# A gated attention block on one core: second-pass output weights loaded a quarter per period, VectorE side work spread anew

## The chip, the cores and the metric

The kernel runs on one core of one Trainium2 chip. Times are device microseconds of that core. The time before is the median of three runs. One further execution was profiled; its trace gives the durations used below. In the trace PE is TensorE (matmuls) and PEld its weight loads, DVE is VectorE, ACT is ScalarE, POOL is GpSimd; SPq is the queue of SyncE, which issues most of the transfers.

## The reference

```python
xn = _layernorm(x)                                  # x: [2048, 640]
# A: 32 heads of 192, the last W = 512 of 2048 cached keys and values
q = xn @ wq                                         # [640, 6144]
p = softmax(q_h @ k_h.T * 192 ** -0.5)              # per head h
s = concat_h(p @ v_h) @ wo                          # [6144, 640]
# B: gated linear unit, 1536 wide
g = silu((sigmoid(xn @ w_gate) * (xn @ w_up)) @ w_down)
return x + s * g
```

Inputs and output are bf16.

## The kernel before

Three stages follow each other, and TensorE works through nearly all of the time.

**Stage B** (about the first 196 us) normalises x and computes g, which is stored to DRAM as `gB_d`.

**Attention** runs in 16 passes `r` = 0 to 15 (`last` = 15). Pass `r` takes two pairs of heads (group `g`) and one half `pi` of the rows, two blocks of 512. In each pass 16 steps `k` compute scores (`stage_s`, L649): six matmuls into one of two PSUM bank pairs, `k % 2` choosing the pair, then one exponential on ACT (L661). So step `k + 2` can't start before the exponential of step `k` has read its banks. Between the steps TensorE does the query projections of the next pass (L571, in `query_slots`), which DVE takes out of PSUM (L592, L605). Then eight `stage_pv` calls (L663) multiply by the values; DVE normalises into `o_st` (L677, L678), a DMA turns it and `store_o` (L691) writes it to `oT_d`. The last pass puts a `stage_pv` behind every second score step, on two PSUM bank pairs.

`phase_s` (L791) is the hand-written schedule of side work in the attention stage: what follows step `k` of pass `r`. It holds the scale factors (`set_scale`, a maximum sent through DRAM to all partitions by two GpSimd transfers, and `set_scale2`, L212, five small DVE instructions that read it back), the sums of absolute values (`abs_v`, L716, on ACT, four per group, one per value tile), and the preparation of the first output weights.

**Output projection** (from about 695 us): `s` is the [2048, 6144] attention output times `wo`. The inner dimension is cut into two halves `h`, 24 chunks of 128 each; h = 0 is the first pass, h = 1 the second. Per half, the product is done by a seven-product scheme on 2 x 2 blocks. The weight side needs seven operands `ops[h][0..6]` of 128 x 3840 elements: four quarters loaded from `wo` (n = 0, 4, 5, 3, by `load_ops`, L696, 960 KB each) and scaled by DVE (`scale_op`, L701), and differences of them (`sum_op`, L704). The row side needs per period four "quads" (A11, A12, A21, A22, 384 KB each, `load_quads`, L760), scaled (L772, ACT) and combined (`sum_quad`, L776, four DVE instructions at L782 to L789).

There are 16 periods `m` (loop at L986): 0 to 7 with h = 0, 8 to 15 with h = 1. A period is seven products of 12 matmuls each (L935), in the order S1, S2, A12, S3, A11 of the next period, S4, A22; the A11 of period 0 stands ahead of the loop. They use the operands 1, 2, 3, 4, 0, 5, 6. Three results per period are added by DVE (L953; L961 and on in the second pass), one is copied by ACT (L942). A product that goes on in a PSUM bank must wait for the DVE result that reads it: A22 of a period waits for the result behind S3.

After a row tile has its first-pass sum in `acc`, `prep` (L921) turns it into x + acc * g in two DVE steps: `gated` (L919, with a row of `gB_d`) and an addition (L927, with a row of x). The two rows, 160 KB each, are brought by `pair_load` (L910) into three pairs of buffers; the second step of a `prep` issues the pair three tiles on. `todo` (L969 to L977) says which scalings, differences and preparation steps a period gets; `side(m, count)` takes `count` of them at five fixed places of the period: two behind S1, one behind S2, one ahead of the S4 result, one behind it, up to four at the end.

All engines run their queues in order, SPq included: at L989 to L994 period 0 issues the quads of period 2, then the four quarters for h = 1, then the first three pairs of gate and x rows.

Of the kernel before, what the change touches and what calls it, by code (L numbers as in the profile page):

```python
# [10 lines left out]
BF16 = mybir.dt.bfloat16  # L11
# [6 lines left out]
def kernel(  # L18
# [13 lines left out]
    nc = tc.nc  # L32
# [660 lines left out]
                oT[:].rearrange("p (q j) e -> p q j e", q=TQ),  # L693
            )

    def load_ops(h):  # L696
        c = 2 * KB * h
        for n, k, d in ((0, 0, LEFT), (4, 0, RIGHT), (5, KB, RIGHT), (3, KB, LEFT)):
            nc.sync.dma_start(ops[h][n].bitcast(BF16), wo_r[:, c + k:c + k + KB, d])  # L699

    def scale_op(h, n):  # L701
        nc.vector.tensor_scalar(ops[h][n], ops[h][n].bitcast(BF16), o_up, None, op0=ALU.mult)

    def sum_op(h, n, part_=None):  # L704
        B11, T1, T2, B21, T3, B22, T4 = ops[h]
        cs = slice(0, KB) if part_ is None else slice(part_ * KB // 2, (part_ + 1) * KB // 2)
        a, b, c = (t[:, cs, :] for t in ((T1, T3, B11), (T2, B22, T1), (T3, B22, T3), (T4, B21, T2))[n])
        nc.vector.tensor_tensor(a, b, c, ALU.subtract)
# [7 lines left out]
    def abs_v(g, n):  # L716
        col = g * NV + n
        nc.scalar.activation(
            v_abs[g // (NG - 1)], v_t[g, n // 2][n % 2][:, :, 0:DH], AF.Abs, accum_out=v_sum[:, col:col + 1])
# [17 lines left out]
    def weights(g, c):  # L737
        scale_w(g, c)
        sum_w(g, c, nc.gpsimd.tensor_tensor, nc.gpsimd.tensor_copy)
        n = g * NCD + c + 3  # L740
        if n < NG * NCD:
            load_raw(n // NCD, n % NCD, nc.gpsimd)
# [48 lines left out]
    def phase_s(r, pi, g, k, q_list, pv_list):  # L791
        for j in q_after.get(k, ()) if q_list else ():
            q_list[j]()
        if r == 0 and k in scale_s:
            scale_raw(1, scale_s[k], on_act=False)
            second_w(scale_s[k])
        if pi == 0 and g + 1 < NG:
            if k == 2 and g > 0:
                load_k((g + 1, 0))
            elif k == 12:  # L800
                scale_k((g + 1, 0))
                load_k((g + 1, 1))
        if pi == 1 and g + 1 < NG:
            if k == 7:
                scale_k((g + 1, 1))
            elif k == 13:
                turn_k((g + 1, 0))
        n = 3 * (g - 1) + k // 2
        if pi == 1 and k == 8:
            for n in range(3 * g, min(3 * g + 3, NWO)):  # L810
                load_wo(n)
        elif pi == 0 and g > 0 and k in (1, 3, 5) and n < NWO:
            abs_wo(n)
        if pi == 1 and g < NG - 1 and k in (1, 3, 4, 5):
            abs_v(g, (1, 3, 4, 5).index(k))
        if r == last - 3 and k == 7:
            set_scale(wo_sum[:], mx_rows[0], mx_o, 1)
        if r == last - 2:
            if k == 7:
                set_scale2(mx_rows[0], mx_o, o_up, o_down)  # L820
            elif k in (9, 11, 13):
                scale_op(0, (0, 4, 5)[(k - 9) // 2])
        if r == last - 1:
            if 5 <= k < 9:
                abs_v(g, k - 5)
            elif k == 10:
                set_scale(v_sum[:], mx_rows[1], mx_v, 2)
            if k in (9, 11, 13):
                sum_op(0, (k - 9) // 4, (k - 9) // 2 % 2)
        if r == last:  # L830
            if k == 0:
                sum_op(0, 1, 1)
            elif k == 2:
                sum_op(0, 2)
            elif k == 13:
                scale_op(0, 3)
            elif k == 14:
                sum_op(0, 3)
            elif k == 4:
                set_scale2(mx_rows[1], mx_v, v_up, v_down)  # L840
                nc.vector.tensor_tensor(descale, v_down, o_down, ALU.mult)
            if k % 2:
                q, x = pv_list.pop(0)
                stage_pv(q, *x)
            if 5 <= k < 9:
                scale_quad(0, ("A21", "A22", "A11", "A12")[k - 5], nc.vector)
            elif 9 <= k < 13:
                sum_quad(0, k - 8)
            if k in (5, 9, 11, 13, 15):
                store_o(1)  # L850

    held = []
    for r, (pi, g) in enumerate(runs):
        s_list = [(i, pp, c) for i in range(2) for pp in range(G) for c in range(KC)]
        pv_list = held + [(r, (i, pp, h)) for i in range(2) for pp in range(G) for h in range(2)]
        q_list = query_slots(r + 1, False, (0, 1), (2, 3), (2, 3, 1)) if r < last else []
        ring[:] = [0, 1, 2, 3]
        bank_order[:] = [1, 0] * 5 if r == last else [0, 1, 2, 3, 0, 2, 1, 0]
        if r == last - 1:
            bank_order[4:] = [1, 0]  # L860
        for k, x in enumerate(s_list):
            stage_s(r, *x, k)
            if k == 0:
                store_o(0 if r < last else 1)
            phase_s(r, pi, g, k, q_list, pv_list)
        if pi == 1 and g + 1 < NG:
            turn_k((g + 1, 1))
        if r == last - 1:
            for m in range(2):
                load_quads(m)  # L870
        if r == last - 1:
            held[:] = pv_list[-2:]
            del pv_list[-2:]
        for k, (q, x) in enumerate(pv_list):
            stage_pv(q, *x)
            if k in (5, 7):
                store_o(2)
            if pi == 0 and 1 <= g < NG - 1 and k in (2, 4):
                weights(g + 1, 2 + k // 2)
            if pi == 1 and g + 2 < NG and k in (1, 3, 5):  # L880
                weights(g + 2, k // 2)
        if pi == 1 and g + 1 < NG:
            for pp in range(G):
                load_v(g + 1, pp, nc.sync)
        if r == last - 3:
            load_ops(0)
    store_o(0)

    lctx.close()
# [31 lines left out]
    def prep(n, step):  # L921
        t = order[n]
        gate, x_sb = gx_rows[0, t]
        if step == 0:
            gated(acc[t][:], acc[t][:], gate)
        else:
            nc.vector.tensor_tensor(acc[t][:], acc[t][:], x_sb, ALU.add)  # L927
            if n + 3 < len(order):
                pair_load(0, n + 3, first)
# [36 lines left out]
        elif (i, d) in ((0, RIGHT), (1, LEFT)):  # L966
            nc.gpsimd.dma_start(of[t * P:(t + 1) * P, :], o_sb)  # L967

    todo = {2: [lambda n=n: scale_op(1, n) for n in (0, 4, 5, 3)]}  # L969
    for m in (3, 4):  # L970
        todo[m] = [lambda n=n: sum_op(1, n) for n in (2 * m - 6, 2 * m - 5)]
    preps = [(n, j) for n in range(2 * 8) for j in range(2)]
    for m, count in {1: 4, 5: 6, 6: 6, 7: 6, 8: 2, 9: 2, 10: 2, 11: 2, 12: 2}.items():
        for _ in range(count):
            n, j = preps.pop(0)
            todo.setdefault(m, []).append(lambda n=n, j=j: prep(n, j))
    assert not preps  # L977

    def side(m, count=1):
# [6 lines left out]
    for m in range(NP):  # L986
        X, Y, Z = (4, 5, 6) if m % 2 == 0 else (0, 1, 2)
        more = m + 1 < NP
        if m + 2 < NP:  # L989
            load_quads(m + 2)  # L990
        if m == 0:
            load_ops(1)
            for n in range(3):
                pair_load(0, n, first)  # L994
        if 8 <= m < NP - 1:
            for i in range(2):
                pair_load(1, 2 * (m - 7) + i, more_rows)
        product(m, Y, "S1", 1, True)
        if more:
            scale_quad(m + 1, "A21", nc.scalar)  # L1000
        keep(Y, p5s[:])
        side(m, 2)
        product(m, X, "S2", 2, False)
        if more:
            scale_quad(m + 1, "A11", nc.scalar)
        keep(X, u2s[:])
        side(m)
        product(m, Z, "A12", 3, True)
        result(m, 0, LEFT, Z, p1s)
        if more:  # L1010
            scale_quad(m + 1, "A22", nc.scalar)
            scale_quad(m + 1, "A12", nc.scalar)
        product(m, X, "S3", 4, False)
        result(m, 1, RIGHT, X, p5s)
        if more:
            sum_quad(m + 1, 1)
            sum_quad(m + 1, 2)
            sum_quad(m + 1, 3)
            product(m + 1, 4 - X, "A11", 0, True)
            keep(4 - X, p1s[:])  # L1020
        side(m)
        product(m, Y, "S4", 5, False)
        result(m, 0, RIGHT, Y, u2s)
        side(m)
        product(m, X, "A22", 6, False)
        result(m, 1, LEFT, X, None)
        if more:
            sum_quad(m + 1, 4)
        side(m, 4)
        if m == 7:  # L1030
            for i in range(2):
                pair_load(1, i, more_rows)
# [29 lines left out]
```

## Time and profile before

| | us |
|---|---|
| median of 3 runs | 893.09 (892.0 to 897.35) |
| profiled execution | 893.61 |
| its span in the trace | 891.8 |
| PE busy | 873.5 (98%) |
| DVE busy | 669.8 (75%) |
| ACT busy | 577.6 (65%) |
| POOL busy | 231.2 (26%) |

The profiled execution took 1.8 us more than its span. By stretches of the span (busy us of each engine, granted TensorE clock, bytes moved):

| stretch, us | PE | DVE | ACT | clock | GB/s |
|---|---|---|---|---|---|
| 200 to 600 (attention) | 400.0 | 295.8 | 316.7 | 1.00 | 180 |
| 690 to 700 | 8.55 | 5.66 | 3.95 | 1.00 | 149 |
| 700 to 710 | 10.00 | 5.00 | 5.97 | 1.00 | 309 |
| 710 to 720 | 7.87 | 0.00 | 5.07 | 1.00 | 323 |
| 720 to 730 | 4.04 | 7.37 | 1.08 | 0.66 | 298 |
| 730 to 740 | 10.00 | 8.18 | 6.84 | 1.00 | 253 |
| 740 to 860 | 120.0 | 102.3 | 77.1 | 1.00 | 200 |

A row of a timeline gives start, length, engine, line, operation, tiles and how many instructions it merges; the bracket says how long the engine stood idle before it and what it waited for. The chain of waits is the path followed back from the last instruction; each row is a stretch of it.

### The profile page before, as it was taken

How to read it: one execution, taken by the hardware profiler on the slowest of the kernel's cores; microseconds unless marked ns; L12 is line 12 of the kernel's file. 1: busy time of each engine (PE TensorE's matmuls, PEld its weight loads, DVE VectorE, ACT ScalarE, POOL GpSimd, SP SyncE). 2: the span in 40 equal slices, each digit the busy share in tenths (PEclk: the TensorE clock that was granted, in tenths of full speed). 3: DMA queues.
4: the chain of work that ended last, by engine and by line, in shares of the span. 5: the costliest groups of instructions: out<-in, count | busy, mean ns of one | idle time of the engine just before them, and what ended most of it. 6: DMA issues, size and time to landing. Idle time of an engine off the chain costs nothing.

```text
span 891.8 us, 18752 instructions
## 1 busy us (share of the span) xinstructions
PE 873.5 (98%) x7576; PEld 564.1 (63%) x7593; DVE 669.8 (75%) x1086; ACT 577.6 (65%) x693; POOL 231.2 (26%) x326
## 2 busy tenths in 40 slices
PE   9999999999999999999999999999999969999998
PEld 5545454557756756766766765775766647777775
DVE  4879947777777777677777777778788458789986
ACT  4333346774896896896896887877456536666662
POOL 0050212662424524523623622621000000000000
PEclk9999999999999999999999999999999989999999
DMA  9993485229799889779979879879977894468641
GB/s 276 270 279 91 106 126 119 83 64 190 130 218 177 150 220 209 126 212 205 170 185 228 150 174 189 153 153 294 174 196 185 249 304 141 131 225 301 194 150 38
DMA packets 246791, 161.34 MB, mean 181 GB/s; under 512 B 158576, under 2 KB 231664, under 8 KB 246704
## 3 DMA queue, kind: packets, MB, share of 16 engines
q1 hardware_dynamic: 238160, 132.90, 61.8%
q0 software_dynamic: 8544, 27.24, 13.9%
q8 instruction: 59, 0.97, 0.5%
q14 instruction: 28, 0.23, 0.1%
HBM read 93.65 MB, written 30.41 MB: 139 GB/s over the span
## 4 chain that ended last, share of the span: by engine, by line
PE 93%; DVE 3%; SPq 2%; DMA 1%; ACT 1%; issue 1%; DVEq 0%; ACTq 0%
PE ps_all L571 20%; PE ps_all L671 19%; PE ps_all L935 19%; PE ps_all L657 18%; PE ps_all L469 11%; PE ps_all L517 6%; SPq L699 1%; PE ps_all L382 1%; DMA kraw<-gB_d 1%; DMA x_sb<-in_A_x_dram 0%; SPq L913 0%; DVE o_st L678 0%; DVE arm L919 0%; ACT E L661 0%; DVE qT L605 0%
## 5 line engine op out<-in xcount | busy, mean ns | idle before, releaser
L661 ACT ACTIVATE E<-ps_all 128x1024 bf16<-128x1024 f32 x256 | 251.6, 1021 | 123.0 <-PE ps_all L657 122.4
L657 PE MATMUL ps_all<-qT,kT 64*128 64x512 bf16 x1536 | 197.6, 376 | 0.6 <-ACT E L661 0.5
L671 PEld LDWEIGHTS <-E 128*128 128x128 bf16 x2048 | 169.5, 98 | 11.4 <-issue 11.4
L671 PE MATMUL ps_all<-v_sb,E 128*128 128x193 bf16 x2048 | 174.9, 247 | 1.4 <-DVE o_st L678 1.4
L605 DVE TENSOR_TENSOR qT<-ps_all,qp 128x512 bf16<-128x512 f32 x176 | 116.9, 688 | 48.3 <-PE ps_all L571 40.8
L592 DVE COPY qp<-ps_all 128x512 f32<-128x512 f32 x150 | 100.6, 687 | 49.4 <-PE ps_all L571 49.4
L657 PEld LDWEIGHTS <-kT 64*128 64x128 bf16 x1536 | 83.7, 94 | 80.3 <-issue 6.0
L935 PEld LDWEIGHTS <-mid 128*128 128x128 f16 x996 | 98.1, 99 | 47.2 <-issue 8.3
L678 DVE TENSOR_TENSOR o_st<-ps_all,rden 128x768 bf16<-128x768 f32 x128 | 122.5, 957 | 4.4
L571 PE MATMUL ps_all<-mid,arm 64*128 64x512 f16 (+1 forms) x840 | 105.7, 376 | 0.6 <-DVE qp L592 0.6
L571 PE MATMUL ps_all<-mid 64*128 64x512 f16 (+1 forms) x840 | 104.5, 376 | 0.6 <-ACT qp L590 0.5
L571 PEld LDWEIGHTS <-mid 64*128 64x128 f16 x840 | 47.8, 94 | 45.0 <-issue 2.0
L571 PEld LDWEIGHTS <-arm 64*128 64x128 f16 x840 | 47.8, 94 | 44.8 <-issue 1.3
L772 ACT ACTIVATE mid<-mid,w_sc 128x1536 f16<-128x1536 bf16 x41 | 63.4, 1571 | 0.0
L967 POOL DMA_DIRECT2D out_dram<-arm x14 | 7.6, 540 | 206.7 <-DVE arm L963 206.7
L240 ACT ACTIVATE mid<-mid,w_sc 128x1536 f16<-128x1536 bf16 x37 | 58.2, 1572 | 0.6
L935 PE MATMUL ps_all<-mid 128*128 128x320 f16 x312 | 46.6, 305 | 8.1 <-DVE acc L953 8.1
L226 POOL DMA_DIRECT2D mid<-in_A_wq_dram x80 | 48.1, 606 | 23.9 <-DVE mid L262 22.4
L474 ACT ACTIVATE sig_sb<-ps_all 128x512 bf16<-128x512 f32 x48 | 28.0, 596 | 40.1 <-PE ps_all L469 37.1
L517 PE MATMUL ps_all<-wd_sb,hT_sb 128*128 128x128 bf16 (+1 forms) x377 | 52.4, 298 | 0.4
L935 PE MATMUL ps_all<-arm,mid 128*128 128x320 f16 x348 | 51.4, 300 | 0.0
L475 DVE TENSOR_TENSOR hT_sb<-ps_all,sig_sb 128x512 bf16<-128x512 f32 x48 | 32.5, 683 | 23.0 <-PE ps_all L469 11.7
(160 smaller groups left out, 1047.4 us busy)
## 6 DMA issues: line engine op xcount, KB each, us to landing
oT_d<-oT SPq DMA_DIRECT2D x64, 384.0 KB, 5.2
mid<-oT_d SPq DMA_DIRECT2D x45, 384.0 KB, 4.0
mid<-in_A_wq_dram POOLq DMA_DIRECT2D x80, 192.0 KB, 6.7
arm<-in_A_wo_dram SPq DMA_DIRECT2D x16, 480.0 KB, 5.8
v_sb<-in_A_v_cache_dram SPq DMA_DIRECT2D x28, 192.0 KB, 6.0
kraw<-in_A_k_cache_dram SPq DMA_DIRECT2D x26, 192.0 KB, 4.1
mid<-in_A_wq_dram POOLq DMA_DIRECT2D x9, 480.0 KB, 6.7
kT<-oT_d SPq DMA_DIRECT2D x11, 384.0 KB, 4.5
```

Of the source, the lines that this page charges most:

```text
L240: nc.scalar.activation(raw.bitcast(F16), raw, AF.Copy, scale=w_up)
L469: nc.tensor.matmul(gu[:, i, :], lhsT=w[:, c, f * P:(f + 1) * P], rhs=xnT[s][:, c, :], start=(c == 0), stop=(c == NCD - 1),)
L517: nc.tensor.matmul(oB_ps[:, d0:d0 + dsz], lhsT=hT_sb[:, f, q * P:(q + 1) * P], rhs=wd_sb[:, f, d0:d0 + dsz], start=(f == 0), stop=(f == NF ...
L571: nc.tensor.matmul(ps_all[:, b, :], lhsT=w(r, c), rhs=x[r, c, :], start=(first and k == 0), stop=(k == len(cs) - 1), skip_group_check=True,)
L592: nc.vector.tensor_copy(dst, part(b))
L605: nc.vector.tensor_tensor(q_out(i, u, pp), part(b), t, ALU.add)
L657: nc.tensor.matmul(ps[:, b, :], lhsT=kT[h, c * PC + j, :], rhs=qT_t[r][i, j][h, pp, :], start=(j == 0), stop=(j == PC - 1),)
L661: nc.scalar.activation(E_t[r, i, pp][:, c, :, :], ps, AF.Exp, scale=scale_qk)
L671: nc.tensor.matmul(o_ps[:, q // 2, q % 2, 0:DH + 1], lhsT=E[:, c, h, q * P:(q + 1) * P], rhs=vt[:, c, 0:DH + 1], start=(c == 0), stop=(c = ...
L678: nc.vector.tensor_tensor(o_st[:, :, h * DH:(h + 1) * DH].rearrange("p (b i) d -> p b i d", b=2), o_ps[:, :, :, 0:DH], rden[:].to_broadcas ...
L772: eng.activation(t, t.bitcast(BF16), AF.Copy, scale=v_up)
L935: nc.tensor.matmul(ps_all[:, b, 0:DN], lhsT=a[:, c, :], rhs=w[:, c, :], start=(start and c == 0), stop=(c == KB - 1), skip_group_check=True,)
```

## The change

The four quarters for h = 1 are no longer issued together in period 0: `load_op(h, j)` issues one, and periods 0 to 3 call it once each, behind the quads and, in period 0, behind the first gate and x rows. Their scaling moves from period 2 (all four) to periods 2, 3, 4 and 5, one each; the four differences from periods 3 and 4 (two each) to periods 4, 5, 6 and 7. The 32 preparation steps, before 4, 6, 6, 6, 2, 2, 2, 2, 2 in periods 1, 5, 6, 7, 8, 9, 10, 11, 12, become 4, 4, 4, 2, 2, 4, 4, 1, 1, 2, 2, 1, 1 in periods 1 to 13.

In the attention stage `set_scale2` for the weights moves from step 7 to step 0 of pass 13; the four `abs_v` of pass 14 move from steps 5 to 8 to steps 3 to 6; and the scaling and difference that make `ops[0][3]` and `ops[0][6]` move from steps 13 and 14 of pass 15 to behind that pass's last `stage_pv`. The first pass's weights are loaded as before. No instruction is added or removed.

```diff
-    def load_ops(h):
-        c = 2 * KB * h
-        for n, k, d in ((0, 0, LEFT), (4, 0, RIGHT), (5, KB, RIGHT), (3, KB, LEFT)):
-            nc.sync.dma_start(ops[h][n].bitcast(BF16), wo_r[:, c + k:c + k + KB, d])
+    op_parts = (0, 0, LEFT), (4, 0, RIGHT), (5, KB, RIGHT), (3, KB, LEFT)
+
+    def load_op(h, j):
+        n, k, d = op_parts[j]
+        c = 2 * KB * h + k
+        nc.sync.dma_start(ops[h][n].bitcast(BF16), wo_r[:, c:c + KB, d])
...
         if r == last - 2:
-            if k == 7:
+            if k == 0:
                 set_scale2(mx_rows[0], mx_o, o_up, o_down)
...
         if r == last - 1:
-            if 5 <= k < 9:
-                abs_v(g, k - 5)
+            if 3 <= k < 7:
+                abs_v(g, k - 3)
...
-            elif k == 13:
-                scale_op(0, 3)
-            elif k == 14:
-                sum_op(0, 3)
...
+        if r == last:
+            scale_op(0, 3)
+            sum_op(0, 3)
         if pi == 1 and g + 1 < NG:
             for pp in range(G):
                 load_v(g + 1, pp, nc.sync)
         if r == last - 3:
-            load_ops(0)
+            for j in range(len(op_parts)):
+                load_op(0, j)
...
-    todo = {2: [lambda n=n: scale_op(1, n) for n in (0, 4, 5, 3)]}
-    for m in (3, 4):
-        todo[m] = [lambda n=n: sum_op(1, n) for n in (2 * m - 6, 2 * m - 5)]
+    todo = {2 + j: [lambda n=part_[0]: scale_op(1, n)] for j, part_ in enumerate(op_parts)}
+    for n in range(4):
+        todo.setdefault(4 + n, []).append(lambda n=n: sum_op(1, n))
     preps = [(n, j) for n in range(2 * 8) for j in range(2)]
-    for m, count in {1: 4, 5: 6, 6: 6, 7: 6, 8: 2, 9: 2, 10: 2, 11: 2, 12: 2}.items():
-        for _ in range(count):
-            n, j = preps.pop(0)
+    for m, count in enumerate((0, 4, 4, 4, 2, 2, 4, 4, 1, 1, 2, 2, 1, 1)):
+        for n, j in preps[:count]:
             todo.setdefault(m, []).append(lambda n=n, j=j: prep(n, j))
+        del preps[:count]
...
         if m == 0:
-            load_ops(1)
             for n in range(3):
                 pair_load(0, n, first)
+        if m < len(op_parts):
+            load_op(1, m)
```

## The prediction, made before the changed kernel had run

> **What bounds the kernel now.** The page first: TensorE is busy for 98% of the span and 93% of the chain that ended last is PE, so only a gap of TensorE, or work that makes one, changes the time. The stretches (table above) leave one place, 690 to 730. The chain of waits in order of time, columns start, length, what, shows it:
>
> ```profile
> 688.06 1.21 DVE mid L702
> ...
> 690.35 2.07 DVE mid L708
> ...
> 693.56 1.49 PE ps_all L671 x16
> 695.05 9.79 PE ps_all L935 x72
> 704.87 0.45 ACT p1s L942
> 705.32 1.25 SPq L699
> 706.56 0.05 issue
> 706.61 4.23 SPq L699
> 710.89 3.65 SPq L699
> 714.53 0.04 issue
> 714.58 3.08 SPq L913
> ...
> 719.13 5.06 DMA kraw<-gB_d
> ```
>
> The end hangs on DVE's scaling and difference at 688 to 692, and then on SPq: three of the four quarters (L699) keep it for 10 us, and the gate rows (L913) wait behind them. The timeline has what TensorE lost:
>
> ```profile
> 619.82 1.26 PE L571 MATMUL ps_all<-mid,arm 64*128 64x512 f16 x10 [0.61 <-DVE qp L592]
> ...
> 693.56 1.49 PE L671 MATMUL ps_all<-v_sb,E 128*128 128x193 bf16 x16 [1.45 <-DVE o_st L678]
> ...
> 722.56 0.89 DVE L919 SCALAR_TENSOR_TENSOR acc<-acc,w_sc,v_sb 128x640 f32<-128x640 f32 x1 [14.71 <-DMA v_sb<-gB_d]
> ...
> 725.96 3.36 PE L935 MATMUL ps_all<-mid 128*128 128x320 f16 x12 [8.09 <-DVE acc L953]
> 729.11 3.83 PE L935 MATMUL ps_all<-arm,mid 128*128 128x320 f16 x24
> ```
>
> Three gaps: 0.61, 1.45 and 8.09 us. The third is one in-order queue: DVE stands at L919 (the first `gated`) for 14.71 us, the result that A22 of period 1 needs is queued behind it, and TensorE waits. After it the granted clock is 0.51 in 726 to 730: the next three products take from 725.96 to 732.77, 6.81 us, against 4.89 at the steady 1.63 of one product (starts at 734.40, 736.03, 737.66). That is 1.92 more. From there to 860 TensorE has no gap.
>
> **Gate rows ahead of the quarters.** The last quad of period 0 leaves SPq at 703.04; with 1.45 us won before, 701.6. The first gate row follows at once. Gate rows took 5.1 to 7.9 us to land, so it is there at 706.7 to 709.5. When must it be? A22 of period 1 is due at 716.08 + 1.63 - 1.45 = 716.3, and DVE has two `gated` (0.88), one addition (0.82) and two results (0.49) before it, 3.56: the row may land as late as 712.7. Three microseconds of cover even with the slowest row, so I take the whole gap and its slow clock as gone, 8.09 + 1.92 = 10.0. If the row took the 11.5 us of a quarter, 0.4 would be left.
>
> **Quarters later.** Quarter j is now issued in period j behind that period's quads and scaled two periods on, at its start. A period is 11.41 us (the ACT copies that end it stand at 752.53, 763.95, 775.36), so 22.8 less some 4 for the issue are left; quarters landed after 8.4 to 11.5. Cost nothing, with 7 us to spare. SPq: quads of period 3 move ahead of three quarters, while quads of later periods get a quarter and up to four rows behind or before them. One period then moves four quads of 393 KB, one quarter of 983 KB and four rows of 164 KB, 3.21 MB in 11.41 us, 281 GB/s; period 0 moves 3.54 MB, 310 GB/s. The stretch moved 311 to 338 GB/s at 710 to 722, so period 0 fits barely and the quads of period 3, due at 718, have about two us of slack behind it.
>
> **DVE's periods.** Every first-pass period has four `sum_quad` (0.95) and three results (0.49), 5.3. With a scaling 1.21, a difference 2.15 and a preparation pair 1.70, the new periods hold: 1: 8.7; 2 and 3: 9.9; 4 and 5: 10.3; 6 and 7: 10.8. From 8 on the base is 9.4 (three results of 0.49 + 0.55 + 0.49, one of 0.54 + 0.49, the quads' 3.8); one or two steps make 10.3 to 11.1, and 11.1 is what periods 8 to 12 had without a gap. All stay under 11.41. Periods 6 and 7 have the least cover of the new ones; the longest block ahead of a result is 3.4 (scaling and difference in 4 and 5), and period 3 had 4.3 before without a gap. Cost nothing, up to 1 a period if the cover fails.
>
> **Last `scale_op` and `sum_op` of the first pass.** L702 and L708 leave DVE ahead of the `o_st` that TensorE waited for; without them `o_st` ends at about 691.95 and the next `stage_pv` is due at 692.1. The 1.45 go. They now stand behind the last `o_st`, 694.8 to 698.2. The scaled quarter is wanted by the fourth product, 693.6 + 3 x 1.63 = 698.5 (done 696.0), the difference by the eighth, 705.0, and the first result behind them is due at 700.6. Covered by 2.4 us; without cover it would cost the same 1.5.
>
> **`set_scale2` at step 0 of pass 13.** Five instructions, 0.96 us, leave a DVE that was late at 619. The 0.61 go. In the new place DVE stood idle for 1.33 us (before the L592 at 605.85), and the row it reads was issued by GpSimd at 596.31 and lands 3.7 us later, 600.0, 4.5 us ahead. Cost nothing.
>
> **`abs_v` two steps earlier.** This adds a wait. The value tiles of the last group are loaded only after pass 13:
>
> ```profile
> 641.20 3.41 SPq L177 DMA_DIRECT2D v_sb<-in_A_v_cache_dram  x4
> 641.98 1.02 ACT L661 ACTIVATE E<-ps_all 128x1024 bf16<-128x1024 f32 x1 [0.70 <-PE ps_all L657]
> 643.77 1.02 ACT L661 ACTIVATE E<-ps_all 128x1024 bf16<-128x1024 f32 x1 [0.76 <-PE ps_all L657]
> ...
> 646.35 0.83 ACT L718 ACTIVATE mid<-v_sb 128x768 bf16<-128x768 bf16 x1
> ```
>
> Step 3's exponential ends at 643.0; the first tile took 4.3 us, so it lands at 645.5. ACT stands 2.5 us with the exponential of step 4 queued behind. Followed on (0.85 per `abs_v`, 0.95 per exponential, all in before's times): step 4 ends at 647.4, and step 6's matmuls, 646.29 before, overwrite its banks: 1.1 late. ACT then alternates both, 1.8 each, up to step 7; step 8's exponential ends at 653.7, and step 10's matmuls, 652.78 before, start then: 0.9 late. Beyond it ACT needs 0.95 a step against TensorE's 1.73 and catches up. Ends: 2.5 if TensorE loses all that ACT does; -0.5 if the tiles land in time, since before step 10 had a wait of 0.47 of this sort. I take 0.9, followed through the queue. Here a rule speaks against the edit. The Trainium skill, "DMA: Bandwidth & Descriptors", Rules for kernel authors, says to issue a transfer early and wait for it late; moving the reader forward does the opposite. The same page ("Anatomy of one DMA") gives 2.0 us + bytes / 436e3, fitted to GpSimd's transfers; for 192 KB that is an estimate of 2.5 us, the tile would be there at 643.7 and the loss nearly nothing, 11.9 or so off in all. The trace's 4.3 for this very transfer decides.
>
> **The sum.** 0.61 + 1.45 + 10.0 - 0.9 = 11.2 off 893.61 (span 891.8 and 1.8 around it) is 882.4. The median of before is 0.5 below the profiled execution: 882.0.
>
> **Rivals.** (1) *Gates still late.* Transfers already under way (stores, quads) hold the rows back beyond 712.7, and part of the third gap stays. For it: the transfer engines are at a share of 0.98 to 1.16 in 698 to 722. Against: the rows landed in 5.1 to 7.9 in that very crowd. A row 15 us late leaves 4 us: 886. A page bears on the clock alone: by "TensorE: Matmul & The Clock Gate", Part 1, only idle time above about 3.4 us drops the clock; here 1.45 left it at 1.00 and 8.09 did not, and no row lies between.
>
> (2) *DVE becomes the bound* in periods 4 to 7, where differences and preparations meet. 10.3 to 10.8 of 11.41 are taken; if handovers eat the rest, four periods lose 0.5 to 1: 884 to 886.
>
> (3) *Transfers become the bound: slower.* Place: periods 0 to 3, where quarters now run beside quads and rows instead of in TensorE's gap. If the queue brings less than 281 GB/s, the quads come late, ACT can't scale them, and TensorE waits each period. It decides at 223 GB/s: 14.4 us a period, four times 3.0, eats 12; at 210 GB/s the kernel takes about 897. For it: 740 to 760 moved only 138 GB/s. Against: that was all that was asked; the full stretches moved 311 and more.
>
> That the change doesn't do what it says can be left aside: both instruction lists hold the same instructions per engine, and the gates stand ahead of the first quarter.
>
> **Numbers.** About 1% (9 us; 884.2) is what a measurement here tells from no change. Forecast, 881 to 884: 0.80. Rival 1: 0.10. Rival 2: 0.06. Rival 3: 0.04. Low end 880.0: no cost for `abs_v` and before's best run, 892.0. High end 886.0: rivals 1 and 2. Faster: 0.80 + 0.06 from rivals that cost little = 0.86; slower 0.03 of rival 3; the rest within 1%.
>
> **What would show it.** No PE gap at L671 near 692 and none beside L953 in period 1; clock 1.00 in 690 to 740; L919's first wait under 3 us; SPq with L913 before the first quarter; ACT waiting 2 to 2.5 us for `v_sb` in pass 14, and about 1 us of PE gaps at L657 behind it. Wrong: a wait of DVE for `arm` or `op` at a scaling, of ACT at L772 for quads, or PE gaps of A22 in periods 4 to 7.

## The result and the profile after

The changed kernel takes 881.46 us (median of 4 runs, 881.04 to 882.14) against 893.68 for the kernel before (4 runs, 892.0 to 897.35): a ratio of 0.9858, 95% interval 0.9827 to 0.989. Its profiled execution took 881.57 with a span of 879.8, 12.0 shorter than the span before.

The list of TensorE's waits from pass 13 to the end (who waited for whom, us in total, times, longest) had four lines before, 8.1, 1.4, 0.6 and 0.5 us. After the change one is left:

```profile
PE ps_all L657 <- ACT E L661: 1.2, 1, 1.2
```

The stretches (columns: from and to, length, busy us and count of PE, PEld, DVE, ACT, POOL, then the granted clock, the share of the transfer engines, GB/s) show 690 to 730 filled and the clock full:

```profile
690.00:700.00 10.00, 10.00 (x90) 7.98 (x88) 6.70 (x8) 5.47 (x7) 0.00 (x0) 1.00 0.78 186
700.00:710.00 10.00, 10.00 (x75) 7.20 (x74) 7.49 (x10) 5.97 (x8) 0.00 (x0) 1.00 1.04 337
710.00:720.00 10.00, 10.00 (x76) 7.22 (x74) 7.62 (x11) 5.97 (x8) 0.00 (x0) 1.00 1.09 367
720.00:730.00 10.00, 10.00 (x76) 7.19 (x75) 7.01 (x11) 5.97 (x7) 0.00 (x0) 1.00 0.92 303
```

The timeline of SPq and DVE at the start of the projection answers to the rows of L699, L913 and L919 before. Lines have moved by two: L915 is the gate row, L917 the x row, L701 a quarter, L768 a quad, L921 `gated`:

```profile
701.26 0.50 SPq L915 DMA_DIRECT2D v_sb<-gB_d  x1
...
704.97 0.33 SPq L917 DMA_DIRECT2D kraw<-in_A_x_dram  x1
706.06 0.38 SPq L701 DMA_DIRECT2D arm<-in_A_wo_dram  x1
706.99 3.39 SPq L768 DMA_DIRECT2D mid<-oT_d  x4
707.48 0.88 DVE L921 SCALAR_TENSOR_TENSOR acc<-acc,w_sc,v_sb 128x640 f32<-128x640 f32 x1 [1.49 <-DMA v_sb<-gB_d]
```

The six rows leave within some 4 us, one quarter follows, then the quads of period 3. DVE's wait for the first gate row fell from 14.71 to 1.49 us, and no PE gap follows it. In the chain of waits (start, length, what) one row stands where the kernel before left TensorE at 704.84 and came back to it at 725.96:

```profile
693.19 177.68 PE ps_all L937 x1308
```

From the first product to 870.87 the chain is TensorE alone. The last 8.9 us of the span are the second pass's last results on DVE, as long as before.

What is new stands in pass 14, in the timeline of ACT and PE:

```profile
644.69 0.84 ACT L720 ACTIVATE mid<-v_sb 128x768 bf16<-128x768 bf16 x1 [2.76 <-DMA v_sb<-in_A_v_cache_dram]
...
645.53 1.00 ACT L661 ACTIVATE E<-ps_all 128x1024 bf16<-128x1024 f32 x1
...
646.59 0.82 PE L657 MATMUL ps_all<-qT,kT 64*128 64x512 bf16 x6 [1.18 <-ACT E L661]
```

The first `abs_v` waits 2.76 us for its value tile, the exponential of step 4 comes behind it, and step 6's matmuls wait 1.18 for that.

### The profile page after: what moved, and what is told of

It reads as the page before. It is cut to its first block, busy times and chain, and to the rows that moved or that the text cites. A ratio compares the mean times of both kernels' runs of the same rounds, so it can differ in the third digit from the quotient of the medians.

```text
span 879.8 us, 18750 instructions
## 1 busy us (share of the span) xinstructions
PE 870.9 (99%) x7576; PEld 563.3 (64%) x7593; DVE 669.7 (76%) x1086; ACT 577.2 (66%) x693; POOL 231.1 (26%) x326
## 4 chain that ended last, share of the span: by engine, by line
PE 97%; ACT 1%; DVE 1%; DMA 0%; issue 0%; SPq 0%; DVEq 0%
PE ps_all L571 20%; PE ps_all L937 20%; PE ps_all L671 20%; PE ps_all L657 19%; PE ps_all L469 11%; PE ps_all L517 6%; PE ps_all L382 1%; ACT E L661 0%; DMA x_sb<-in_A_x_dram 0%; ACT mid L720 0%; DVE arm L921 0%; DVE arm L965 0%; ACT qp L590 0%; DVE arm L963 0%; DVE qT L605 0%
## 5 line engine op out<-in xcount | busy, mean ns | idle before, releaser
L671 PEld LDWEIGHTS <-E 128*128 128x128 bf16 x2048 | 169.5, 98 | 9.9 <-issue 9.8
L671 PE MATMUL ps_all<-v_sb,E 128*128 128x193 bf16 x2048 | 174.9, 247 | 0.0
L937 PE MATMUL ps_all<-op,mid 128*128 128x320 f16 x336 | 48.2, 299 | 0.0
```

The costliest lines, as they stand in the source:

```text
L671: nc.tensor.matmul(o_ps[:, q // 2, q % 2, 0:DH + 1], lhsT=E[:, c, h, q * P:(q + 1) * P], rhs=vt[:, c, 0:DH + 1], start=(c == 0), stop=(c = ...
L937: nc.tensor.matmul(ps_all[:, b, 0:DN], lhsT=a[:, c, :], rhs=w[:, c, :], start=(start and c == 0), stop=(c == KB - 1), skip_group_check=True,)
```

## The experiments

Up to pass 13 all kernels here are the same program, yet pass 13 starts anywhere from 602.8 to 604.0 us in their traces. So a difference of a microsecond between two medians can lie ahead of the change. Each trace was therefore cut at the same four instructions: the first score matmul of passes 13, 14 and 15, and the first product; the last stretch ends with the span. All in us, from the start columns of the PE timelines:

| kernel | pass 13 | pass 14 | pass 15 | projection | median of runs |
|---|---|---|---|---|---|
| before | 33.73 | 31.00 | 26.91 | 196.9 | 893.68 |
| changed | 32.80 | 31.73 | 25.39 | 186.8 | 881.46 |
| a1_order_alone | 33.73 | 31.00 | 26.91 | 194.1 | 891.67 |
| a2_quarters_first | 32.81 | 31.51 | 25.39 | 197.1 | 892.16 |
| a3_abs_back | 32.81 | 31.00 | 25.39 | 186.8 | 880.63 |
| a4_tail_back | 32.80 | 31.60 | 26.91 | 186.8 | 882.82 |
| b1_scale2_back | 33.74 | 31.49 | 25.40 | 186.8 | 882.38 |
| b2_four_behind | 32.80 | 31.27 | 25.39 | 193.1 | 888.84 |
| b3_two_ahead | 32.80 | 31.37 | 25.40 | 188.5 | 882.97 |
| b4_old_preps | 32.80 | 31.76 | 25.39 | 187.4 | 882.80 |
| b5_two_a_period | 32.80 | 31.30 | 25.39 | 186.8 | 881.57 |
| c1_abs_spread | 32.80 | 30.63 | 25.39 | 186.8 | 880.53 |

A stretch that an edit doesn't touch repeats to 0.01 or 0.1; pass 14 with the early `abs_v` varies by 0.5, since it depends on when a transfer lands. The kernel before was run again beside each group of experiments: 893.92 beside a1 to a4, 894.92 beside b1, b2, b4 and c1, 893.81 beside b3 and b5.

**a1_order_alone**: the kernel before with only the order in period 0 changed.

```diff
-            load_ops(1)
             for n in range(3):
                 pair_load(0, n, first)
+            load_ops(1)
```

> The kernel before with one swap: in period 0 the three pairs of gate and x rows are issued ahead of the four quarters; nothing else of the change. Theory O (the whole 10 us came from the order of gates and quarters on SPq; the quarter per period and the new spread over DVE add nothing): the third gap is gone and nothing takes its place, 893.7 - 10 = 883.7, clock 1.00 in 690 to 740. Theory S (the spread is needed as well): the quads of period 3 now stand behind 3.9 MB of quarters, 12 us at some 320 GB/s; ACT waits for them in period 2, and TensorE loses 2 to 4 us there: 885.5 to 888. I hold S, with the larger part of the gain from the order. The gaps of 0.61 and 1.45 us in the attention stage stay in both.

Measured: 891.67, ratio 0.9976 (0.9953 to 1.0). Of the 10.1 us of the projection only 2.8 were won, not the larger part that was expected. Its timeline:

```profile
710.32 0.88 DVE L919 SCALAR_TENSOR_TENSOR acc<-acc,w_sc,v_sb 128x640 f32<-128x640 f32 x1 [1.87 <-DMA v_sb<-gB_d]
...
717.66 4.47 SPq L766 DMA_DIRECT2D mid<-oT_d  x4
...
725.94 1.57 ACT L772 ACTIVATE mid<-mid,w_sc 128x1536 f16<-128x1536 bf16 x1 [5.37 <-DMA mid<-oT_d]
...
729.86 3.36 PE L935 MATMUL ps_all<-mid,k_sb 128*128 128x320 f16 x12 [4.87 <-ACT u2s L942]
733.01 2.64 PE L935 MATMUL ps_all<-arm,mid 128*128 128x320 f16 x12
735.49 1.79 PE L935 MATMUL ps_all<-mid 128*128 128x320 f16 x12
```

The gate wait is gone (1.87), but the quads of period 3 now leave SPq at 717.66; counted from the first product that is 8.2 us later than in the changed kernel (22.2 against 14.0). ACT waits 5.37 us to scale the first, its copies out of PSUM are queued behind, and TensorE waits 4.87 for one of them. The mechanism is theory S. The size was above it: the gap alone is 4.87 where 2 to 4 were expected, and the slow clock was left out. Two products from 729.86 to 735.49 take 5.63 instead of 3.26, 2.4 more. 4.87 + 2.4 = 7.2 of the 7.3 that are missing.

**b2_four_behind**: the changed kernel with all quarters in period 0, behind the rows.

```diff
-        if m < len(op_parts):
-            load_op(1, m)
+            for j in range(len(op_parts)):
+                load_op(1, j)
```

> The changed kernel with all four quarters issued in period 0, behind the gate and x rows: the quarter per period is undone, the spread over DVE stays. Theory S1 (the lump of quarters delays the quads of period 3, whatever DVE does): as in the swap alone, ACT waits some 5 us for a quad in period 2, TensorE some 5 with a slow clock after it, 881.5 + 7 to 8 = 888.5 to 890. Theory S2 (it was the old burst of four scalings in period 2, waiting for the last quarters, that cost the time in the swap alone): with one scaling a period the loss is gone, 881.5 to 883.

Measured: 888.84, the projection 6.4 longer than in the changed kernel, with DVE's work spread as in the change:

```profile
722.86 1.57 ACT L774 ACTIVATE mid<-mid,w_sc 128x1536 f16<-128x1536 bf16 x1 [5.32 <-DMA mid<-oT_d]
...
726.77 3.21 PE L937 MATMUL ps_all<-mid,k_sb 128*128 128x320 f16 x12 [4.80 <-ACT u2s L944]
```

ACT waited 5.3 us for the quad and TensorE 4.8; the product after the gap took 3.04 instead of 1.63. So it is the lump of quarters on the queue, S1. The projection of a1 is 1.0 longer still (194.1 against 193.1), which is the longer loss to the slow clock there (2.4 against 1.4); of DVE's old burst the two show no cost.

**a2_quarters_first**: the changed kernel with all quarters ahead of the rows, as before.

```diff
         if m == 0:
+            for j in range(len(op_parts)):
+                load_op(1, j)
             for n in range(3):
                 pair_load(0, n, first)
-        if m < len(op_parts):
-            load_op(1, m)
```

> The changed kernel with all four quarters issued in period 0 ahead of the gate and x rows, as before the change; the new spread over DVE and the three edits in the attention stage stay. If the order of the queue is the cause, the wait of the first gated step (some 15 us) and the PE gap of 8 us beside period 1 are back, with the slow clock behind it: 881.5 + 10 = 891.5. If the new spread of DVE's work is what removed the gap, a good part stays away: under 887.

Measured: 892.16; the projection takes 197.1, against 196.9 before. The gap is back as it was, whatever DVE's spread:

```profile
720.87 0.88 DVE L921 SCALAR_TENSOR_TENSOR acc<-acc,w_sc,v_sb 128x640 f32<-128x640 f32 x1 [14.77 <-DMA v_sb<-gB_d]
...
724.26 3.36 PE L937 MATMUL ps_all<-mid 128*128 128x320 f16 x12 [8.14 <-DVE acc L955]
```

**b3_two_ahead**: two quarters ahead of the rows, the others in periods 1 and 2.

```diff
         if m == 0:
+            for j in range(2):
+                load_op(1, j)
             for n in range(3):
                 pair_load(0, n, first)
-        if m < len(op_parts):
-            load_op(1, m)
+        if m in (1, 2):
+            load_op(1, m + 1)
```

> The changed kernel with two quarters issued ahead of the first gate and x rows in period 0, the others in periods 1 and 2. DVE's wait for the first gate row was 1.5 us with none ahead and 14.8 with four: 3.3 a quarter. Two should make it 8.1, the row landing some 1.5 to 1.8 us behind the latest time that the prediction worked out (712.7 there, 712.3 in the changed kernel's own times). Theory of the deadline: a PE gap of 1.5 to 2 us in front of A22 of period 1, without a fall of the clock, and the stretch from the first product to the end 1.6 longer than the 186.8 of the changed kernel: 188.4, time near 883. Rival (any wait of DVE there passes to TensorE in full): 6.6 us, 888.

Measured: 882.97, the projection 1.8 longer. DVE waited 8.28 us and TensorE 1.66; the clock stayed at 1.00 in 714 to 726. Of DVE's wait 6.6 were cover. In this run's times the prediction's latest time is 711.8 (its first product starts 0.5 earlier than the changed kernel's); the first `gated` starts at 713.82, 2.0 behind it, and TensorE lost 1.7 to 1.8. The deadline holds within 0.3 us.

```profile
713.82 0.88 DVE L921 SCALAR_TENSOR_TENSOR acc<-acc,w_sc,v_sb 128x640 f32<-128x640 f32 x1 [8.28 <-DMA v_sb<-gB_d]
...
717.21 1.79 PE L937 MATMUL ps_all<-mid 128*128 128x320 f16 x12 [1.66 <-DVE acc L955]
```

**b5_two_a_period**: two quarters each in periods 0 and 1, behind the rows.

```diff
-        if m < len(op_parts):
-            load_op(1, m)
+        if m < 2:
+            for j in range(2):
+                load_op(1, 2 * m + j)
```

> The changed kernel with the four quarters in two periods, two each, behind the rows. In the changed kernel the first quad of period 3 lands near 714.1 and ACT takes it at 718.0, 3.9 us of cover; one more quarter ahead of it is 3.1 to 3.3 us. Theory (cover of the quads sets how many quarters may go together: one more fits, three more did not): no loss, 186.8 from the first product to the end, 881.5. Rival (one quarter a period is the most that the queue carries): ACT waits 1 us or more at the quads of period 3 or 4 and TensorE loses 1 to 4: 882.5 to 885.5.

Measured: 881.57, projection 186.8, no wait of ACT for quads. One quarter a period is more caution than is needed; four at once are too many.

**b4_old_preps**: the old counts of preparation steps, all else as changed.

```diff
-    for m, count in enumerate((0, 4, 4, 4, 2, 2, 4, 4, 1, 1, 2, 2, 1, 1)):
+    for m, count in enumerate((0, 4, 0, 0, 0, 6, 6, 6, 2, 2, 2, 2, 2)):
```

> The changed kernel with the preparation steps back at 4, 6, 6, 6 and five times 2 in periods 1 and 5 to 12; quarters, scalings and differences as changed. By the sums DVE then has 13.8 us in period 5 and 12.6 in 6 and 7 against 11.41: 2.4 + 1.2 + 1.2 = 4.8 too much. Theory D (DVE binds there, so the new spread of the preparations is needed once the differences are late): 881.5 + 2 to 4.8, with PE gaps beside L955 in periods 5 to 7. Rival (results run ahead far enough to absorb it): 881.5.

Measured: 882.80 (881.62 to 884.21), the projection 0.6 longer. DVE was full for three slices on end, and TensorE without a gap beside it:

```profile
760.00:770.00 10.00, 10.00 (x76) 7.19 (x75) 9.91 (x12) 6.91 (x8) 0.00 (x0) 1.00 0.41 103
770.00:780.00 10.00, 10.00 (x76) 7.22 (x74) 9.92 (x13) 5.97 (x8) 0.00 (x0) 1.00 0.64 220
780.00:790.00 10.00, 10.00 (x76) 7.19 (x74) 9.90 (x14) 5.97 (x8) 0.00 (x0) 1.00 0.72 239
```

The products start late only at 796.14 and 798.13, by 0.2 and 0.4 against the steady 1.63. Nearly the rival: of 4.8 us too much work 0.6 came through. DVE had room before it, 7.62 busy in 750 to 760. What did come through stands just ahead of those two products, where DVE had waited 2.00 us for a gate row of the second pass (`gated` at 794.58) and ACT 1.52 for a quad (796.46). SPq had issued that period's gate rows only from 790.93, against 786.88 in the changed kernel, and the quads behind them: an x row ahead of them left at 790.55, when the preparation step that frees its buffer had ended (789.70 + 0.82). So a late DVE shows at the queue; this is read from the trace and not tested apart.

**a3_abs_back** and **c1_abs_spread**: the `abs_v` of pass 14 at their old steps, and spread over steps with room.

```diff
-            if 3 <= k < 7:
-                abs_v(g, k - 3)
+            if 5 <= k < 9:                      # a3
+                abs_v(g, k - 5)
...
+            for n in {5: (0,), 6: (1, 2), 10: (3,)}.get(k, ()):   # c1
+                abs_v(g, n)
-            elif k == 10:
+            if k == 12:                         # c1: set_scale
```

> The changed kernel with the four abs_v of pass 14 back at steps 5 to 8. Theory of the prediction (ACT's wait for the value tile costs TensorE some 0.9 us, net of the 0.47 wait that the old place had): ACT has no wait for v_sb, the PE gap of 1.18 us at L657 is gone, one of about 0.5 comes back near step 10, and the time is 0.5 to 0.9 lower, 880.6 to 881.0. Rival (what ACT loses is hidden, TensorE makes it up within the pass): no change, 881.5.

> The changed kernel with the abs_v of pass 14 at steps 5, 6 (two, where TensorE has two query products in the step) and 10, and the maximum that needs them at step 12 instead of 10. With steps 5 to 8 the kernel took 880.63 and TensorE still waited 0.47 us for ACT near step 10. If ACT's load is the cause, that wait goes too: 880.2. Rival: ACT has no more slack at step 10 and the wait only moves (880.6), or the later maximum makes DVE wait for it at step 4 of pass 15 (over 880.8).

Measured: 880.63 and 880.53. In a3 ACT doesn't wait for the tile (an exponential ends just before `abs_v` at 645.08), and pass 14 has its 31.00 of before with the wait of 0.47; in c1 that wait is gone too and the pass takes 30.63. By the stretches c1 is 1.1 us faster than the changed kernel and 0.4 faster than a3; the medians can't tell a3 and c1 apart. Both are shorter than the kernel before (c1: ratio 0.9839, 0.9807 to 0.9871), and by pass 14 than the changed kernel; the runs of c1 (880.36 to 881.65) overlap with those of the changed kernel (881.04 to 882.14).

**a4_tail_back** and **b1_scale2_back**: one edit of the attention stage undone each.

```diff
+            elif k == 13:                       # a4
+                scale_op(0, 3)
+            elif k == 14:
+                sum_op(0, 3)
...
-        if r == last:
-            scale_op(0, 3)
-            sum_op(0, 3)
```

```diff
-            if k == 0:                          # b1
+            if k == 7:
                 set_scale2(mx_rows[0], mx_o, o_up, o_down)
```

> The changed kernel with the scaling and the difference for ops[0][3] and ops[0][6] back at steps 13 and 14 of pass 15. Theory of the prediction: the 1.45 us gap of TensorE before the last stage_pv is back, 881.5 + 1.5 = 883.0. Rival (the late start of the projection is absorbed by the wait for the gate rows, which now stand at the edge: DVE waited 1.5 us for the first): DVE's wait at the first gated step shrinks and TensorE loses the 1.5 all the same, since that wait cost it nothing; or, if the gates do bind, under 882.

> The changed kernel with set_scale2 for the weights back at step 7 of pass 13. Prediction: the 0.61 us gap at L571 is back, 882.1. From the two traces (pass 14 starts 1.07 us earlier after the change, 0.14 of which it had at the start of pass 13) the move is worth 0.9, since the bracket of the gap leaves out what the modelled end of the matmul ahead hides: 882.4. Rival (the time is made up within the pass): 881.5.

Measured: 882.82 and 882.38. In a4 pass 15 has its 26.91 back, with the 1.45 gap at L671, and the projection is no shorter: DVE's wait for the gate row had been cover. In b1 pass 13 has its 33.74 back, 0.94 more than without:

```profile
618.00 1.47 PE L657 MATMUL ps_all<-qT,kT 64*128 64x512 bf16 x12
620.08 1.26 PE L571 MATMUL ps_all<-mid,arm 64*128 64x512 f16 x10 [0.60 <-DVE qp L592]
621.15 1.48 PE L657 MATMUL ps_all<-qT,kT 64*128 64x512 bf16 x12
622.60 1.26 PE L571 MATMUL ps_all<-mid,arm 64*128 64x512 f16 x10
```

From 618.00 to 620.08 are 2.08 us; the same step takes 1.30 in the changed kernel. That is 0.78 where the bracket says 0.60: the bracket counts from the modelled end of the matmuls ahead, and without any wait that end lies 0.18 behind the next start (in the changed kernel 617.60 + 1.48 = 619.08 against 618.90). The next pair, 621.15 to 622.60, takes 1.45 instead of 1.29 and has no bracket at all.

## Why the prediction was right

The total came out as summed: 11.2 off were predicted, 12.0 measured between the two spans. 0.1 of it lies ahead of pass 13. The terms:

- *Gates ahead of the quarters*, 10.0: 196.91 - 186.77 = 10.14. a2 brings the whole of it back. The latest time for the gate row, worked out from DVE's 3.56 us of work ahead of A22, was tested by b3: the row came 2.0 us behind it and left 1.66 us of gap.
- *Quarters later*, nothing: right. The cover of the quads of period 3 was given as about two us; the first quad landed 7.1 us after its issue at 706.99, 714.1, and was scaled at 718.0, so it was 3.9. The prediction saw this edge but not that the gain hangs on it: the new order without the quarter per period (a1, b2) keeps only 2.8 to 3.8 of the 10.1. The 8.4 to 11.5 us that it gave a quarter to land are medians of groups; single ones before took 7.3 to 12.2, and the outcome doesn't hang on it.
- *DVE's periods*, nothing: right. b4 puts up to 2.4 us too much into a period and loses 0.6 in all, where rival 2 put 0.5 to 1 on each of four periods.
- *Last `scale_op` and `sum_op`*, 1.45: 26.91 - 25.39 = 1.52, and a4 gives it back.
- *`set_scale2`*, 0.61: the mis-sized term. It was read from a gap's bracket and is 0.93, as b1 shows.
- *`abs_v`*, a cost of 0.9: 0.73 by the stretches (31.73 - 31.00), between 0.3 and 0.8 over the kernels that have it. The wait for the tile was 2.76 where 2.5 was expected, TensorE's gap 1.18 where 1.1 was. The estimate of 2.5 us for the transfer, from the Trainium skill, "DMA: Bandwidth & Descriptors", Anatomy of one DMA, did not hold for this transfer, which SyncE issues: it took 4.5. The rule to wait late, from the same page's Rules for kernel authors, did hold: a3 and c1, which wait later, have the lowest medians.
- *The rivals.* Gates too late: b3 shows the beginning of it, a2 the whole. Transfers as the bound did not come about in the changed kernel; b2 and a1 show it in the form of quads behind a lump of quarters.

What isn't tried: how many of the first rows' six transfers need to stand ahead of the quarter, and whether the quads of period 3 could go ahead of the rows as well.

## What to carry to other kernels

In an in-order issue queue, order transfers by the time at which their reader would hold up the bound engine: subtract the reader's own queued work from that engine's deadline, and compare with the landing times in the same traffic. Bulk that is wanted late does harm twice, ahead of what is wanted now and, moved behind that, ahead of what is wanted next; so move it behind and cut it up in the same step. To size effects under a microsecond, cut the traces at fixed instructions and compare stretches: here they repeat to 0.1 us or better, where medians of the kernel before scatter by one.

## What the runs showed of the hardware

The granted clock went with the length of TensorE's idle time: 1.45 and 1.66 us left it at 1.00, 4.80 and 4.87 brought it down, as 8.09 did. The windows behind the gap of 4.8 in b2 and behind that of 4.87 in a1 show how it comes back:

```profile
722.00:726.00 4.00, 0.00 (x0) 0.00 (x0) 0.49 (x1) 3.08 (x3) 0.00 (x0) 1.00 1.05 387
726.00:730.00 4.00, 3.23 (x14) 1.84 (x14) 0.00 (x0) 3.64 (x4) 0.00 (x0) 0.57 1.05 397
730.00:734.00 4.00, 4.00 (x31) 2.88 (x30) 3.89 (x5) 0.44 (x1) 0.00 (x0) 1.00 0.22 76
```

```profile
726.00:730.00 4.00, 0.14 (x1) 0.10 (x1) 0.00 (x0) 3.93 (x5) 0.00 (x0) 0.74 1.05 383
730.00:734.00 4.00, 4.00 (x16) 2.21 (x15) 0.68 (x2) 2.73 (x2) 0.00 (x0) 0.50 0.97 373
734.00:738.00 4.00, 4.00 (x29) 2.76 (x27) 3.97 (x6) 0.44 (x1) 0.00 (x0) 0.91 0.46 119
```

The clock was at half while it was down. So a window's time at half clock is twice what its mean lacks of 1.00, and over the windows this sums to about 3.4 us in b2 and 6.8 in a1; the clock records of the traces say 3.41 and 6.83, with 6.83 in the kernel before and 10.24 in a2. These are one, two and three times one length.

Only the part of it that falls on work costs anything. TensorE had restarted 2.9 us before the clock came back in b2, 4.0 in the kernel before, 4.2 in a2 and 4.9 in a1. Half of that is 1.5, 2.0, 2.1 and 2.4; the products behind the gap lost 1.4, 1.9, 2.0 and 2.4. So nearly the same gap, 4.80 and 4.87, cost 1.4 in one run and 2.4 in the other.

The lengths agree with the Trainium skill, "TensorE: Matmul & The Clock Gate", Part 1, which describes a window of 3.4 us that runs free of the kernel. The prediction cites the same part for a fall only behind more than about 3.4 us of idle time. Here the measurement differs: in a2 the clock fell at 718.18, 2.1 us after the modelled end of TensorE's last matmul. So 3.4 us isn't a safe length for a gap; between 1.66 and 4.80 us no gap of these runs lies.
